# The opening of an agent-attention and expand-contract kernel, put in another order

## The chip, the cores and the metric

One of the eight cores of a Trainium2 chip runs the whole program. The metric is device time: microseconds from the start of the program to its end on that core. A time of a kernel is the median over several executions; one more execution is recorded by the hardware profiler, and all times inside the program come from that one.

A core has five engines with an instruction queue each, all in order: TensorE (PE in the profile; its weight loads have a row of their own, PEld), VectorE (DVE), ScalarE (ACT), GpSimd (POOL) and SyncE (SP), which here does nothing but start transfers. Sixteen DMA engines move the data.

## What is computed

Four batches; 12480 tokens of 128 numbers in each, 49 agents. First attention through the agents, then a layer that widens to 2048 and comes back:

```
s = scale * (a @ b.T);  e = exp(s - max(s));  sm(a, b) = e / (sum(e) + 1e-9)
agent_v = sm(agents, k) @ v                # 49 x 128 for each batch
x = sm(q, agents) @ agent_v                # one row for each token
h = x @ w_in                               # 128 -> 2048
out = (h - tanh(h)) @ w_out                # 2048 -> 128
```

`w_in` and `w_out` come as 64-bit floats and are turned into 32-bit floats on the chip ("decoding": six VectorE instructions and one on ScalarE for 512 columns).

## The kernel before

The inner products are reordered: `agent_v @ w_in` is made once for each batch (49 x 2048, "projection"), so that h is a product of the 49 weights of a token with it. h has 100 blocks of up to 500 tokens (`blocks`), and each block takes eight steps (`steps`, 256 of the 2048 columns each), 800 in all. A step is: `m1` (L563, h into PSUM, six matmuls), `tanh` and `square` on ScalarE (L573, L578), `mul` on VectorE (L583, g = h·z, which stands for h - tanh(h) at small h), and `m2` (L632, g times its part of w_out, added up in PSUM over the eight steps). In about two thirds of the steps g is split into a high part (GpSimd, L613) and a rest (VectorE, L618), so that `m2` can use fast 32-bit matmuls, twelve of them; the steps named in `PLAIN`, and all of block 0, take `m2` with g as it is, in eight passes of the slower form. Keys and values of batches 1 to 3 are worked on between the steps of the batch before; those of batch 0 have to come first. That is the opening, and it is what the change is about:

1. *Loads.* `fast` makes a list `loads`, and SP starts it in that order: 13 key tiles (`kt`, 512 KB each but the last) with the four parts of w_in (`raw`, 512 KB) in between, the first queries, 13 value tiles (`vt`), the second queries and the four parts of w_out. Keys and values share eight buffers (`K0`), so value tile j waits until TensorE is done with the tile that had its buffer. After the loads SP starts the small copies `pb<-pT` (L551, L552) that the first `m1` needs.
2. *Scores of batch 0* (`scores(g)` with b == 0, L273): eight 128-token tiles for a group, each a matmul with 128 columns of keys as weights and the agents of two batches, 98 columns, as the moving side; of those, 49 are used. ScalarE copies them (L284), VectorE takes the maxima (L286). In between VectorE decodes w_in (L175 to L185).
3. *Maximum* over all tokens (L314 to L334).
4. *Exponentials and values* (`av(g)`): VectorE subtracts the maximum (L344), ScalarE takes the exponential (L349), TensorE multiplies with the values (L380), and VectorE adds the exponentials up in two sums, one for even and one for odd groups (L399), added to each other at the end (L402). The first queries' softmax (`q_softmax`: L508, L514 to L529) and their transposition (L538, L547) stand in between.
5. *Quotient* (`sums`: L415 to L422) and the first parts of the projection (L472 to L476), among them, on VectorE, half of the decoding of the first part of w_out.
6. *Block 0*: its eight steps with the rest of the decoding of w_out and of the projection between them. Later in block 0 and at the start of block 1 `split_w_out` makes high and low parts of w_out, one quarter at each of the four positions in `SPLIT`: copies on ScalarE (L213, L218), difference on GpSimd (L214).

Order: VectorE and ScalarE run in the order in which the code is written from the end of the scores on (`issue_order(..., at)`), GpSimd and TensorE from the mark `early` on. Loads before `early` go first on SP.

The end: after the last block `low(0)` and `out` finish the last step, `take` and `finish` add the two halves of the result, and the last transfer carries blocks 98 and 99 together (L809).

Of the kernel before, what the change touches and what calls it, by code (L numbers as in the profile page):

```python
# [24 lines left out]
A = 49  # L25
# [9 lines left out]
GT = 8  # L35
# [29 lines left out]
SPLIT = (7, 4, 6, 8)  # L65
# [37 lines left out]
class Build:  # L103
# [95 lines left out]
    def load_w_in(self, c, raw):  # L199
        tiles = (self.work.tile([128, 512], F32, tag=t, name=t, bufs=2) for t in ("de", "rem", "da", "db"))  # L200
        run(self.decode(raw, self.w_in[:, c * 512 : (c + 1) * 512], *tiles))
# [6 lines left out]
    def split_w_out(self, c):  # L208
# [4 lines left out]
        nc.scalar.copy(h, w)  # L213
        nc.gpsimd.tensor_tensor(l, w, h.bitcast(F32), ALU.subtract)  # L214
        nc.gpsimd.memset(self.vb[c][:, :, C : C + 1], 1.0)
        for i, t in self.wo_f.items():
            if c == i // 2:
                nc.scalar.copy(t, w[:, 2 * C * (i % 2) :][:, : 2 * C])  # L218

    def phase1(self, b):  # L220
# [36 lines left out]
        def scores(g):  # L257
            yield
            if g == 0:
                st["s"] = self.keep.tile([128, NG * (GT + 1) * A], F32, tag="s", name="s", bufs=1)  # L260
                if b == 0:
                    st["mxp"] = self.work.tile([128, A, 2 * NG], F32, tag="mxp", name="mxp", bufs=1)
# [7 lines left out]
            if b == 0:  # L270
                ps = self.banks("h")
                for t in range(n):
                    nc.tensor.matmul(  # L273
                        ps[:, t // 4, (t % 4) * A2 : (t % 4 + 1) * A2],
                        kt[:, t, :],
                        self.ag[:, 0:2, :],
                        start=True,
                        stop=True,
                    )
                pv = ps[:, :, : 4 * A2].rearrange("p c (t a) -> p c t a", a=A2)[:, :, :, :A]  # L280
                for c in range(-(-n // 4)):
                    m = min(4, n - 4 * c)
                    sl = slice((g * GT + 4 * c) * A, (g * GT + 4 * c + m) * A)
                    nc.scalar.copy(st["s"][:, sl].rearrange("p (t a) -> p t a", a=A), pv[:, c, :m])  # L284
                banks = -(-n // 4)
                nc.vector.tensor_reduce(  # L286
                    st["mxp"][:, :, 2 * g : 2 * g + banks].rearrange("p a c -> p c a"),
                    pv[:, :banks, : min(4, n)].rearrange("p c t a -> p c a t"),
                    axis=AX.X,
                    op=ALU.max,  # L290
                )
                if g == EARLY - 1:
                    nc.vector.tensor_reduce(
                        st["mxp"][:, :, 2 * NG - 1], st["mxp"][:, :, : 2 * EARLY], axis=AX.X, op=ALU.max
                    )
                return
            ps = self.misc()
            for t in range(n):
                for r in range(0, 128, QUART):
                    to = ps[r : r + QUART, t * A : (t + 1) * A]  # L300
                    nc.tensor.matmul(to, kt[:, t, r : r + QUART], self.ag[:, b, :], start=True, stop=True)  # L301
            yield
            here = st["s"][:, g * GT * A : (g * GT + n) * A]
# [5 lines left out]
        def max_in():  # L309
# [3 lines left out]
            part = st["mxp"] if b else st["mxp"][:, :, 2 * EARLY :]  # L313
# [23 lines left out]
        def av(g, gaps=(0, 1)):  # L337
# [61 lines left out]
            nc.vector.tensor_tensor(es, e0, flat, ALU.add)  # L399
# [285 lines left out]
    def fast(self):  # L685
# [21 lines left out]
        with ExitStack() as first:  # L707
# [29 lines left out]
            for g in range(NG):  # L737
                run(p1[g])
                load(1)
                if g % 2 == 1 and 2 < g < 11:  # L740
                    self.load_w_in((g - 3) // 2, raws[(g - 3) // 2])
# [27 lines left out]
        early = self.count()  # L769
# [5 lines left out]
        rest0 = p1[2 * NG + 3 :]  # L775
        sums = rest0.pop(0)
        q1 = q_job(1)
        next(q1)
        for _ in range(3):
            next(sums)  # L780
        next(q1)
        go(dec[0], 3)
        run(sums)
        next(q1)
        run(rest0.pop(0))
        go(dec[0], 1)
        run(rest0.pop(0))
# [186 lines left out]
```

## Time and profile before

| what | value |
| --- | --- |
| median of three runs | 2018.5 us (2017.13 to 2018.8) |
| the profiled execution | 2018.59 us, its span 2016.8 us, 1.79 us lie around the span |
| TensorE busy | 1986.9 us of the span (99%) |
| VectorE, ScalarE, GpSimd busy | 1825.6, 1806.5, 999.9 us |
| the first 100 us: TensorE busy | 13.79, 17.81, 16.87, 16.53, 18.94 us in stretches of 20 us |

A row of a timeline reads: start in us, length in us, engine, line of the program, operation, output<-input, shapes, count, and in brackets how long the engine stood idle just before and what ended it. A row of the windows gives a stretch, its length, the busy time of PE, PEld, DVE, ACT and POOL (with counts), the granted TensorE clock as a share of full speed, the busy share of the DMA engines and what they moved in GB/s. A row of the waits reads: who waited, for whom, us in total, how often, the longest.

### The profile page before, as it was taken

The numbers are of one execution on the slowest core, as the hardware profiler recorded it, in microseconds if no ns is written. First come the engines' busy times: TensorE is split into PE (matmuls) and PEld (weight loads), VectorE is DVE, ScalarE is ACT, GpSimd is POOL, SyncE is SP. The second block draws the span as 40 slices with busy tenths as digits, with TensorE's granted clock in tenths as the row PEclk, the third lists the DMA queues.
The fourth block names the chain that finished last, engine by engine and source line by source line (L and its number), as shares of the span: only waits on it lengthen the run. The fifth ranks groups of instructions, "written<-read, shape, count | busy, mean of one in ns | idle before, by whom it ended". The sixth has DMA issues, their size and how long they took to land.

```text
span 2016.8 us, 49577 instructions
## 1 busy us (share of the span) xinstructions
PE 1986.9 (99%) x20779; PEld 1460.9 (72%) x20779; DVE 1825.6 (91%) x1986; ACT 1806.5 (90%) x2052; POOL 999.9 (50%) x702
## 2 busy tenths in 40 slices
PE   8899999999999999999999999999999999999998
PEld 7477767777677777777677777777767777777775
DVE  7799999889999998898999999889899999999997
ACT  3789989899999998899999999998999999999996
POOL 1254455555445455554454454555545546555554
PEclk9899999999999999999999999999999999999999
DMA  9422112221111222221012111221101101101100
GB/s 331 135 85 93 54 45 84 83 61 44 54 61 65 78 71 60 78 75 60 31 36 92 61 58 44 71 61 56 54 29 34 52 31 35 52 29 37 39 24 27
DMA packets 76601, 129.70 MB, mean 64 GB/s; under 512 B 5384, under 2 KB 55376, under 8 KB 76368
## 3 DMA queue, kind: packets, MB, share of 16 engines
q1 hardware_dynamic: 76368, 126.44, 19.2%
q8 instruction: 165, 2.70, 0.6%
q14 instruction: 68, 0.56, 0.1%
HBM read 81.10 MB, written 25.56 MB: 53 GB/s over the span
## 4 chain that ended last, share of the span: by engine, by line
PE 84%; ACT 8%; DVE 4%; issue 2%; DMA 1%; SPq 0%; POOL 0%; DVEq 0%; POOLq 0%
PE acc L632 49%; PE h L563 26%; ACT z L578 4%; ACT y L573 4%; DVE g L583 2%; PE misc L508 2%; PE misc L357 2%; PE pt L538 1%; PE misc L301 1%; PE h L273 1%; DVE gl L618 1%; PE misc L472 1%; DMA v<-w_out 1%; PE h L380 0%; ACT s L349 0%
## 5 line engine op out<-in xcount | busy, mean ns | idle before, releaser
L613 POOL TENSOR_SCALAR gh<-g 128x1000 fp32r<-128x1000 f32 (+1 forms) x545 | 853.0, 1565 | 622.5 <-DVE g L583 578.6
L583 DVE TENSOR_TENSOR g<-h,z 128x1000 f32<-128x1000 f32 (+1 forms) x800 | 955.5, 1195 | 133.5 <-ACT z L578 122.9
L573 ACT ACTIVATE y<-h 128x1000 f32<-128x1000 f32 (+1 forms) x800 | 802.4, 1003 | 68.6 <-PE h L563 60.5
L578 ACT ACTIVATE z<-y 128x1000 f32<-128x1000 f32 (+1 forms) x800 | 831.4, 1039 | 25.4
L618 DVE TENSOR_TENSOR gl<-g,gh 128x1000 fp32r<-128x1000 f32 (+1 forms) x545 | 656.8, 1205 | 1.3 <-POOL gh L613 1.0
L563 PE MATMUL h<-pT,awh 49*128 49x504 f32 x1600 | 552.0, 424 | 0.0
L632 PE MATMUL acc<-g,wo_f 64*128 64x500 f32 (+1 forms) x1960 | 443.3, 578 | 0.0
L632 PE MATMUL acc<-gh,wo_l 64*128 64x500 f32 (+1 forms) x2180 | 433.0, 387 | 0.5 <-POOL gh L613 0.2
L632 PE MATMUL acc<-gh,wo_h 64*128 64x500 f32 (+1 forms) x2180 | 432.6, 386 | 0.0
L563 PE MATMUL h<-pT,awl 49*128 49x504 f32 x800 | 369.5, 462 | 7.2 <-DVE awl L476 3.4
L632 PE MATMUL acc<-gl,wo_h 64*128 64x500 f32 (+1 forms) x2180 | 341.2, 387 | 1.0 <-DVE gl L618 0.5
L563 PE MATMUL h<-pb,awh 49*128 49x504 f32 x1600 | 317.1, 387 | 0.0
L563 PE MATMUL h<-pb,awl 49*128 49x504 f32 x800 | 309.0, 386 | 0.0
L632 PEld LDWEIGHTS acc<-g,wo_f 64*128 64x128 f32 x1960 | 190.6, 186 | 145.3 <-issue 126.1
L563 PEld LDWEIGHTS h<-pT,awh 49*128 49x128 f32 x1600 | 265.9, 186 | 20.9 <-issue 11.1
L632 PEld LDWEIGHTS acc<-gh,wo_h 64*128 64x128 f32 x2180 | 214.3, 186 | 37.2
L632 PEld LDWEIGHTS acc<-gl,wo_h 64*128 64x128 f32 x2180 | 211.5, 184 | 40.0 <-DVE gl L618 5.7
L632 PEld LDWEIGHTS acc<-gh,wo_l 64*128 64x128 f32 x2180 | 211.1, 184 | 38.6 <-POOL gh L613 1.7
L563 PEld LDWEIGHTS h<-pT,awl 49*128 49x128 f32 x800 | 147.6, 184 | 117.4 <-DVE o L641 49.9
L529 POOL TENSOR_TENSOR pp<-qe,pp 128x392 fp32r<-128x392 f32 x50 | 51.5, 1030 | 265.3 <-DVE pp L527 257.2
L563 PEld LDWEIGHTS h<-pb,awh 49*128 49x128 f32 x1600 | 153.9, 184 | 29.9 <-DMA pb<-pT 0.5
L563 PEld LDWEIGHTS h<-pb,awl 49*128 49x128 f32 x800 | 149.3, 187 | 11.7 <-issue 6.4
(113 smaller groups left out, 1130.4 us busy)
## 6 DMA issues: line engine op xcount, KB each, us to landing
kt<-kT SPq DMA_DIRECT2D x48, 512.0 KB
qt<-qT SPq DMA_DIRECT2D x46, 500.0 KB
outT<-o SPq DMA_DIRECT2D x46, 500.0 KB
pb<-pT SPq DMA_DIRECT2D x200, 96.5 KB
v<-v SPq DMA_DIRECT2D x36, 512.0 KB
vt<-v SPq DMA_DIRECT2D x12, 512.0 KB
raw<-w_in SPq DMA_DIRECT2D x4, 512.0 KB
v<-w_out SPq DMA_DIRECT2D x4, 512.0 KB
```

The source lines that it names most:

```text
L273: nc.tensor.matmul(ps[:, t // 4, (t % 4) * A2 : (t % 4 + 1) * A2], kt[:, t, :], self.ag[:, 0:2, :], start=True, stop=True,)
L301: nc.tensor.matmul(to, kt[:, t, r : r + QUART], self.ag[:, b, :], start=True, stop=True)
L357: nc.tensor.matmul(ps[HALF * odd : HALF * odd + w, : C + 1], flat[:r, t * A : t * A + w], vt[:r, t, : C + 1], start=t < 2, stop=t >= n - 2,)
L508: nc.tensor.matmul(to, qt[:, token : token + QUART], self.ag[:, b, :], start=True, stop=True)
L529: nc.gpsimd.tensor_tensor(pp[:, :, HALF:PW], ev, pp[:, :, :A].bitcast(F32), ALU.subtract)
L563: nc.tensor.matmul(h[:, c, : BT * TT], aw[a][rows[c], sl], pT[p][rows[c], :], start=k == 0, stop=k == 2)
L573: self.nc.scalar.activation(self.pair(y), h, AF.Tanh, scale=TSC)
L578: self.nc.scalar.activation(z, y, AF.Square, scale=GSC)
L583: self.nc.vector.tensor_tensor(self.pair(g), h, self.pair(z), ALU.mult)
L613: self.nc.gpsimd.tensor_scalar(gh, g, 1.0, 0.0, ALU.mult, ALU.add)
L618: self.nc.vector.tensor_tensor(gl, g, gh.bitcast(F32), ALU.subtract)
L632: nc.tensor.matmul(acc[:, r, :w], weights(c)[rows], g[rows, c * w : (c + 1) * w], start=i == 0 and k == 0, stop=i == NCH // 2 - 1 and k == ...
```

## The change

- *Scores.* The batch-0 scores are made as those of the other batches are: for each tile four matmuls with 32 tokens of keys as weights and the 49 agents of batch 0. One ScalarE copy and one VectorE maximum of 49 x 8 for a group, straight from PSUM.
- *Loads.* Two parts of w_in go between the keys, the other two between the values. They are decoded after the value products (part 2) and beside the quotient and the first projection (part 3).
- *Sums.* The odd groups' exponentials are added up on GpSimd instead of VectorE (five additions).
- *Quotient first.* Quotient and first projection stand ahead of the decoding of w_out, whose first half now follows them and whose second half comes after the first `mul`.
- *w_out.* The copies of `split_w_out` go from ScalarE to GpSimd, and two of the four positions move later (7 to 8, 8 to 9).
- *End.* Blocks 98 and 99 are stored one by one, and the very last step is a plain one: no high and low part.

Behind the scores the line numbers of the new kernel are 6 to 19 lower. The core of the diff:

```
-SPLIT = (7, 4, 6, 8)
+SPLIT = (8, 4, 6, 9)
...
-        nc.scalar.copy(h, w)
+        nc.gpsimd.tensor_scalar(h, w, 1.0, 0.0, ALU.mult, ALU.add)
...
-                nc.scalar.copy(t, w[:, 2 * C * (i % 2) :][:, : 2 * C])
+                nc.gpsimd.tensor_scalar(t, w[:, 2 * C * (i % 2) :][:, : 2 * C], 1.0, 0.0, ALU.mult, ALU.add)
...
-            if b == 0:
-                ps = self.banks("h")
-                for t in range(n):
-                    nc.tensor.matmul(
-                        ps[:, t // 4, (t % 4) * A2 : (t % 4 + 1) * A2],
-                        kt[:, t, :],
-                        self.ag[:, 0:2, :],
...
             ps = self.misc()
             for t in range(n):
                 for r in range(0, 128, QUART):
                     to = ps[r : r + QUART, t * A : (t + 1) * A]
                     nc.tensor.matmul(to, kt[:, t, r : r + QUART], self.ag[:, b, :], start=True, stop=True)
...
+            if b == 0:
+                nc.scalar.copy(here, ps[:, : n * A])
+                nc.vector.tensor_reduce(
+                    st["mxp"][:, :, g], ps[:, : n * A].rearrange("p (t a) -> p a t", a=A), axis=AX.X, op=ALU.max
+                )
...
-            nc.vector.tensor_tensor(es, e0, flat, ALU.add)
+            (nc.gpsimd if g % 2 else nc.vector).tensor_tensor(es, e0, flat, ALU.add)
...
-                if g % 2 == 0 and 0 < g < 10:
-                    loads.append((load_raw, g // 2 - 1))
+                if g in (2, 5):
+                    loads.append((load_raw, g // 3))
...
+                if g in (4, 8):
+                    loads.append((load_raw, 1 + g // 4))
                 loads.append((self.v0, g))
...
+            run(self.load_w_in(2, raws[2]))
+            early = self.count()
...
+            run(sums)
+            part = rest0.pop(0)
+            go(part, 3)
+            w3 = self.load_w_in(3, raws[3])
+            go(w3, 3)
+            run(part)
+            next(q1)
+            go(w3, 1)
+            run(rest0.pop(0))
+            run(w3)
...
         go(dec[0], 3)
-        run(sums)
-        next(q1)
-        run(rest0.pop(0))
-        go(dec[0], 1)
-        run(rest0.pop(0))
-        run(dec[0])
...
+            if n >= len(blocks) - 2:
+                nc.sync.dma_start(self.outT[:, column(n) : column(n) + width(n)], out_at(n))
...
-            plain = n == 0 or n % 2 * HP + i in PLAIN
+            plain = n == 0 or n % 2 * HP + i in PLAIN or k == len(steps) - 1
...
+            if k == 0:
+                run(dec[0])
...
+            if i == 0:
+                run(part)
```

On SP, the transfers of the opening in the new kernel, from the first keys to the last values (`raw` is a part of w_in):

```order
L235 DMA kt<-kT 128x1024 x2
L190 DMA raw<-w_in 128x512
L235 DMA kt<-kT 128x1024 x3
L190 DMA raw<-w_in 128x512
L235 DMA kt<-kT 128x1024 x7
L235 DMA kt<-kT 128x256
L476 DMA qt_99<-qT 128x1000
L246 DMA vt<-v 128x1024 x4
L190 DMA raw<-w_in 128x512
L246 DMA vt<-v 128x1024 x4
L190 DMA raw<-w_in 128x512
L246 DMA vt<-v 128x1024 x4
```

Before, all four parts of w_in stand among the first eight key tiles. The number of transfers and of bytes up to the last value tile is the same, and w_out and the copies `pb` follow as they did.

On VectorE before, from the last step of the quotient (`av<-avs`) to the second `mul` (`g<-h,z`); `gh`, `gl` and `awh<-gl` are the decoding of w_out here, `awl` the projection:

```order
L451 COPY av_95<-avs 128x49 x2
L476 TENSOR_TENSOR awl<-h,awh 113x256
L181 SCALAR_TENSOR_TENSOR gl<-v_90,gh 128x512
L476 TENSOR_TENSOR awl<-h,awh 113x512
L183 TENSOR_TENSOR gl<-gh,gl 128x512
L185 SCALAR_TENSOR_TENSOR awh<-gl 128x512
L583 TENSOR_TENSOR g<-h,z 128x1000
L175 TENSOR_SCALAR gh<-v_91 128x512
L177 SCALAR_TENSOR_TENSOR gh<-v_91,gh 128x512
L179 TENSOR_SCALAR gh<-gh 128x512
L476 TENSOR_TENSOR awl<-misc,awh 113x512
L583 TENSOR_TENSOR g<-h,z 128x1000
```

And the same place in the new kernel, where `da`, `db`, `rem` are the decoding of the last part of w_in:

```order
L179 TENSOR_SCALAR db<-da 128x512
L457 TENSOR_TENSOR awl<-h,awh 113x256
L496 TENSOR_REDUCE qm<-qe 128x8
L181 SCALAR_TENSOR_TENSOR rem<-raw,db 128x512
L457 TENSOR_TENSOR awl<-h,awh 113x512
L183 TENSOR_TENSOR rem<-da,rem 128x512
L185 SCALAR_TENSOR_TENSOR w_in<-de,rem 128x512
L175 TENSOR_SCALAR gh<-v_90 128x512
L177 SCALAR_TENSOR_TENSOR gh<-v_90,gh 128x512
L179 TENSOR_SCALAR gh<-gh 128x512
L564 TENSOR_TENSOR g<-h,z 128x1000
L181 SCALAR_TENSOR_TENSOR gl<-v_90,gh 128x512
```

The last three instructions of the first part of w_out have moved behind the first `mul`; part 3 of w_in stands where they stood.

On GpSimd in the new kernel, from the first queries' difference (`qe`) on; `es` are the sums of exponentials, `pp` the low part of the first queries' weights, `wo_h`, `wo_l`, `wo_f` the parts of w_out:

```order
L498 TENSOR_TENSOR qe<-qe,qm 128x392
L380 TENSOR_TENSOR es<-s 128x392
L380 TENSOR_TENSOR es<-es,s 128x392 x4
L510 TENSOR_TENSOR pp<-qe,pp 128x8x49
L213 TENSOR_SCALAR wo_h<-awh 128x512
L214 TENSOR_TENSOR wo_l<-awh,wo_h 128x512
L215 MEMSET v_91 128x8
L218 TENSOR_SCALAR wo_f_88<-awh 128x256
L498 TENSOR_TENSOR qe<-qe,qm 128x392
L213 TENSOR_SCALAR wo_h<-awh 128x512
```

Before, `pp` follows `qe` at once, and of each quarter of w_out only `wo_l` and the small fill stand here.

More of the change, by code (lines that the diff above doesn't have):

```diff
@@ L200, in load_w_in @@
         tiles = (self.work.tile([128, 512], F32, tag=t, name=t, bufs=2) for t in ("de", "rem", "da", "db"))
-        run(self.decode(raw, self.w_in[:, c * 512 : (c + 1) * 512], *tiles))
+        return self.decode(raw, self.w_in[:, c * 512 : (c + 1) * 512], *tiles)
     def load_w_out(self, c, raw):
@@ L261, in scores @@
                 if b == 0:
-                    st["mxp"] = self.work.tile([128, A, 2 * NG], F32, tag="mxp", name="mxp", bufs=1)
+                    st["mxp"] = self.work.tile([128, A, NG + 1], F32, tag="mxp", name="mxp", bufs=1)
                 else:
@@ L269, in scores @@
                 ahead("v", load_v, 0, g - NG + vb + 1)
-            if b == 0:
-                ps = self.banks("h")
-                for t in range(n):
-                    nc.tensor.matmul(
-                        ps[:, t // 4, (t % 4) * A2 : (t % 4 + 1) * A2],
-                        kt[:, t, :],
-                        self.ag[:, 0:2, :],
[L277 to L296, printed above, removed]
             ps = self.misc()
@@ L301, in scores @@
                     nc.tensor.matmul(to, kt[:, t, r : r + QUART], self.ag[:, b, :], start=True, stop=True)
+            here = st["s"][:, g * GT * A : (g * GT + n) * A]
+            if b == 0:
[3 more added lines that the diff above has]
+                )
+                if g == EARLY - 1:
+                    nc.vector.tensor_reduce(st["mxp"][:, :, NG], st["mxp"][:, :, :EARLY], axis=AX.X, op=ALU.max)
+                return
             yield
-            here = st["s"][:, g * GT * A : (g * GT + n) * A]
             nc.scalar.copy(here, ps[:, : n * A])
@@ L312, in max_in @@
             m = self.small.tile([128, A], F32, tag="m", name="m")
-            part = st["mxp"] if b else st["mxp"][:, :, 2 * EARLY :]
+            part = st["mxp"] if b else st["mxp"][:, :, EARLY:]
             nc.vector.tensor_reduce(m, part, axis=AX.X, op=ALU.max)
@@ L739, in fast @@
                 load(1)
-                if g % 2 == 1 and 2 < g < 11:
-                    self.load_w_in((g - 3) // 2, raws[(g - 3) // 2])
+                if g in (3, 7):
+                    run(self.load_w_in(g // 4, raws[g // 4]))
             at = self.count() - 1
@@ L768, in fast @@
                 run(av[g])
-        early = self.count()
+            run(self.load_w_in(2, raws[2]))
+            early = self.count()
+            rest0 = p1[2 * NG + 3 :]
+            sums = rest0.pop(0)
+            q1 = q_job(1)
+            next(q1)
+            for _ in range(3):
+                next(sums)
+            next(q1)
+            run(sums)
[4 more added lines that the diff above has]
+            run(part)
+            next(q1)
+            go(w3, 1)
+            run(rest0.pop(0))
+            run(w3)
         self.main = ExitStack()
@@ L774, in fast @@
         dec = [self.load_w_out(c, raws[4 + c]) for c in range(4)]
-        rest0 = p1[2 * NG + 3 :]
-        sums = rest0.pop(0)
-        q1 = q_job(1)
-        next(q1)
-        for _ in range(3):
-            next(sums)
-        next(q1)
-        go(dec[0], 3)
-        run(sums)
-        next(q1)
-        run(rest0.pop(0))
-        go(dec[0], 1)
-        run(rest0.pop(0))
-        run(dec[0])
+        go(dec[0], 3)
         live = []
```

2 lines of the change are left out of this document (1 added, 1 removed).

## The prediction

> **What bounds the kernel now.** First the windows, for where TensorE is full, and then the opening in windows of 4 us, for the DMA engines (last two columns: share, GB/s) and the granted clock (third from the end):
>
> ```profile
> 400.00:1000.00 600.00, 599.18 (x6353) 435.01 (x6351) 549.61 (x589) 547.14 (x616) 305.81 (x214) 1.00 0.20 62
> ...
> 32.00:36.00 4.00, 2.45 (x69) 2.04 (x71) 2.40 (x8) 0.65 (x2) 0.00 (x0) 0.64 1.03 406
> 36.00:40.00 4.00, 4.00 (x40) 4.00 (x42) 3.25 (x6) 2.25 (x6) 1.09 (x1) 0.51 0.37 86
> 40.00:44.00 4.00, 4.00 (x78) 4.00 (x75) 4.00 (x10) 3.95 (x10) 0.00 (x0) 1.00 0.89 288
> 44.00:48.00 4.00, 3.08 (x58) 2.84 (x54) 3.90 (x8) 0.52 (x1) 1.12 (x1) 1.00 0.94 315
> ...
> 56.00:60.00 4.00, 3.98 (x10) 1.73 (x10) 1.47 (x3) 0.96 (x2) 0.00 (x0) 0.50 1.03 266
> ...
> 64.00:68.00 4.00, 1.44 (x8) 1.19 (x10) 3.66 (x6) 3.94 (x6) 0.00 (x0) 0.90 0.52 170
> ```
>
> In the long stretch TensorE is full (599.18 of 600 us), and the change takes no work from it. So only the two ends can move: until TensorE is full, and after it has run dry. What reaches the full stretch earlier comes out of the total one for one. In the opening the DMA engines are full (1.03, 406 GB/s) but for a dip from 36 to 40 us, and not quite full to 48. The waits say why; the chain of waits and the timelines of TensorE and ScalarE say what hangs on it:
>
> ```profile
> SPq L246 <- PE h L380: 9.0, 5, 6.1
> ...
> PEld h L563 <- DMA pb<-pT: 0.5, 1, 0.5
> ...
> 46.64 12.14 DMA v<-w_out
> ...
> 59.85 0.74 PE L563 MATMUL h<-pb,awh 49*128 49x504 f32 x2
> ...
> 60.63 1.01 ACT L573 ACTIVATE y<-h 128x1000 f32<-128x1000 f32 x1 [1.11 <-PE h L563]
> ```
>
> Value tiles wait for TensorE to free a buffer, one of them 6.1 us: the dip. The last part of w_out lands at 46.64 + 12.14 = 58.78 us. The small copies `pb`, queued after it, land right behind: the first `m1` waits for them, its last matmuls begin at 59.85, and the first tanh at 60.63. So block 0 starts when the DMA queue has worked itself out. From there on VectorE is full, with `mul`s and decoding, as the window from 64 us shows (3.66 of 4; TensorE 1.44).
>
> **The change part by part.**
>
> *Scores.* TensorE's rows: the old form; the new form as batch 1 has it (64 instructions are a group of eight tiles); the same form at low clock; and VectorE's first subtraction:
>
> ```profile
> 6.21 25.15 PE L273 MATMUL h<-ag,kt 128*128 128x98 f32 x196 [6.21 <-DMA kt<-kT]
> ...
> 116.72 0.88 PE L301 MATMUL misc<-ag,kt 128*32 128x49 f32 x64
> ...
> 34.39 1.53 PE L508 MATMUL misc<-ag,qt 128*32 128x49 f32 x64
> ...
> 34.74 1.04 DVE L344 TENSOR_TENSOR s<-s,mb 128x392 f32<-128x392 f32 x2
> ```
>
> 196 instructions are 12.25 groups: 2.05 us a group now, 0.9 to 1.5 in the new form. A tile of 128 x 1024 x 4 bytes takes 1.29 us at 406 GB/s, so now the keys' arrival sets the pace. At 6.21 us the agents and the first tile are there; the other keys and two parts of w_in are 6.9 MB, another 17 us: TensorE ends at about 24, not at 31.36. Next late are the maxima on VectorE, new form (as batch 1 takes it, from SBUF) and old form (from PSUM):
>
> ```profile
> 118.66 0.87 DVE L305 TENSOR_REDUCE s<-s 128x49 f32<-128x392 f32 x1
> ...
> 15.81 0.56 DVE L286 TENSOR_REDUCE mxp<-h 128x98 f32<-128x392 f32 x1
> ```
>
> With 0.87 each and two parts of w_in decoded between them (six instructions each, at most 0.68 us as `L181` below) VectorE catches up from behind and ends some 1.5 us after TensorE. The Trainium skill (TensorEngine Tiling (Array Packing), Performance Considerations) warns of this: tiling speeds up TensorE and not the emptying of PSUM, which may become the bound. The trace agrees in so far as 0.87 us stand against the 1.29 of an arrival; with 0.56 the stage would end about a microsecond sooner, and nothing below would change.
>
> From TensorE's end to the first subtraction it is 34.74 - 31.36 = 3.4 us. So that comes at about 28.5 us (26.5 to 30, by the two prices), 6.2 earlier. The value tile that waited 6.1 us will find its buffer free while earlier transfers, the two late parts of w_in among them, still fill the engines to about 37 us: **the dip goes**. Its worth: against 406 GB/s there are missing 320 x 4, 118 x 4 and, to the last value at about 46.5 us, 91 x 2.5 us: 2.0 MB or 4.9 us. By the shares of the dip alone it would be 0.63 x 4 = 2.5. I take the bytes, since bytes are what must arrive, less something for the slowest engine: `pb` and the first tanh come **4.5 us earlier**, at 56.1 (bounds 2.5 and 5.0).
>
> *What else could hold the first tanh.* TensorE's last value products now, and the first projection:
>
> ```profile
> 48.64 2.53 PE L380 MATMUL h<-vt,s 128*64 128x128 f32 x36
> ...
> 56.02 2.88 PE L472 MATMUL h<-w_in,av 128*113 128x256 f32 x4 [1.47 <-DVE av L451]
> ```
>
> Up to the last value 14.9 MB follow the first key tile, 37 us: 43. From the end of the products to the projection it is 56.02 - 51.17 = 4.9 us, and less with the quotient first. The second queries' scores (1.53 us at low clock) stand ahead of the projection on TensorE and wait for a load that is two transfers behind the last value, 46 to 47. With 2.88 us for the projection that makes 43 + 4.9 + 1.5 + 2.9 = 52.3 at most, some 3 us before `pb`: covered. Under this cover lie also the two parts of w_in decoded late, and the five additions on GpSimd, priced by its nearest row:
>
> ```profile
> L529 POOL TENSOR_TENSOR pp<-qe,pp 128x392 fp32r<-128x392 f32 x50 | 51.5, 1030 | 265.3 <-DVE pp L527 257.2
> ```
>
> 5 x 1.03 = 5.2 us ahead of `pp` in GpSimd's queue. Begun at 31 they end before 37; the transposition that waits for `pp` stands behind the tenth value tile, at 41 or so. What VectorE is spared there nobody waits for. If `pb` were early and the cover gone, the late decoding would cost about 2 us.
>
> *Block 0 on VectorE.* From the first `mul` to the seventh, and one decoding instruction alone and beside GpSimd's work:
>
> ```profile
> 62.74 1.20 DVE L583 TENSOR_TENSOR g<-h,z 128x1000 f32<-128x1000 f32 x1 [1.17 <-ACT z L578]
> ...
> 74.29 0.68 DVE L181 SCALAR_TENSOR_TENSOR gl<-v,gh 128x512 f32<-128x512 uint32 x1
> ...
> 80.41 1.18 DVE L181 SCALAR_TENSOR_TENSOR gl<-v,gh 128x512 f32<-128x512 uint32 x1
> ...
> 82.96 2.30 DVE L583 TENSOR_TENSOR g<-h,z 128x1000 f32<-128x1000 f32 x2
> ```
>
> That is 20.2 us. Three more decoding instructions move in, 3 x 0.68 = 2.0, and about half of it goes into VectorE's own gaps there: **+1.0** (0 to 2). While VectorE waits for `pb` the order does not let it decode.
>
> *w_out's copies.* ScalarE loses eight; GpSimd's price for a copy is that of `gh`, alone and beside VectorE:
>
> ```profile
> L213 ACT CAST wo_h<-awh 128x512 fp32r<-128x512 f32 x4 | 2.4, 606 | 0.0
> L218 ACT COPY wo_f<-awh 128x256 f32<-128x256 f32 x4 | 1.5, 401 | 0.0
> ...
> 94.71 1.02 POOL L613 TENSOR_SCALAR gh<-g 128x1000 fp32r<-128x1000 f32 x1 [2.26 <-DVE g L583]
> 96.10 1.92 POOL L613 TENSOR_SCALAR gh<-g 128x1000 fp32r<-128x1000 f32 x1 [0.36 <-DVE g L583]
> ...
> 86.68 1.20 DVE L583 TENSOR_TENSOR g<-h,z 128x1000 f32<-128x1000 f32 x1
> ...
> 87.07 0.52 ACT L527 CAST pp<-qe 128x392 fp32r<-128x392 f32 x1
> ...
> 92.25 0.56 ACT L644 COPY o<-acc 128x500 f32<-128x500 f32 x1
> ...
> 92.84 0.68 DVE L641 TENSOR_TENSOR o<-o,acc 128x500 f32<-128x500 f32 x1 [2.05 <-ACT o L644]
> ...
> 93.57 0.49 PE L563 MATMUL h<-pT,awl 49*128 49x504 f32 x1 [0.78 <-DVE o L641]
> ```
>
> TensorE gets its full stretch at 93.57, 10.6 us behind the seventh `mul`, held by ScalarE. Without the copies the way is: two `mul`s and the second queries' quotient on VectorE, 86.68 - 82.96 = 3.7; then their cast 0.5, which ScalarE now waits for; four activations of 1.0; the result's halves 0.6 and 0.7: 9.5. So **-1.1** (0 to -3.9, all eight copies). On GpSimd a quarter of w_out costs its copies, 512 and 256 wide, 0.5 to 1.0 and 0.25 to 0.5, more than before, and three quarters run beside decoding. There they collide, as `L181` with 1.18 for 0.68 and `gh` with 1.92 for 1.02 show. Three such hits, less the one that is there now: **+1.0** (0 to 3.5, if seven were hit). The Trainium skill (GPSIMD Engine Reference, 1. Specifications) has the rule: GpSimd's way to SBUF is shared with VectorE and contends with its instructions that read two SBUF inputs. It speaks against this part, and both pairs of rows bear it out.
>
> *The end.*
>
> ```profile
> 2004.55 1.15 DVE L618 TENSOR_TENSOR gl<-g,gh 128x960 fp32r<-128x960 f32 x1
> ...
> 2007.79 0.73 PE acc L632 x4
> ...
> 1994.32 1.78 PE L632 MATMUL acc<-g,wo_f 64*128 64x480 f32 x8
> 1995.56 0.77 PE L563 MATMUL h<-pT,awl 49*128 49x504 f32 x1
> ...
> 2009.82 0.34 SPq L809 DMA_DIRECT2D outT<-o  x1
> ```
>
> The last step's plain form needs only its g. The step before it ends at 2005.70 + 0.73, then come 1.24 us (start to start of the plain rows): 2007.7 instead of 2008.5. The last transfer carries 480 columns instead of 980; 250 KB less at 406 GB/s are 0.6 us of the 7.0 from its start to the end of the span. Together **-1.4** (-0.8 to -2.2).
>
> *Sum:* -4.5 + 1.0 - 1.1 + 1.0 - 1.4 = -5.0 us. The profiled execution, 2018.59, becomes 2013.6; it lies 0.09 above the median of the runs shown, so the median is forecast at 2013.5. A change of 0.2%, 4.0 us, is about what a measurement of this kernel can tell from none; so "faster" begins below 2014.5, and the forecast lies only a microsecond beyond it.
>
> **The rivals.**
>
> *The dip only moves.* The value tile's wait of 6.1 us falls by what the first subtraction gains. Should the thirteen maxima and the twelve decoding instructions each take 0.17 us longer than priced, VectorE is 4.2 us later, the subtraction gains 2 us and not 6.2, and by the shares 2.5 x 2 / 6.1 = 0.8 us of the opening is left: 3.7 us more, 2017.2. For it: VectorE is the slow engine there, and w_out's rows move only 266 GB/s at a full share (56 to 60), so bytes may promise too much. Against it: VectorE has some 1.29 us for each arrival. Chance 0.24.
>
> *`pb` is not held behind w_out.* The copies are small and spread over few of the sixteen DMA engines; landing right behind w_out now may be chance. Then the projection, at about 52.3, sets the first tanh: 53.1, 7.5 us earlier, 3.0 more than forecast: 2010.5. For it: nothing but their size; against it: 58.78 and 59.85 lie only 1.1 us apart. Chance 0.13.
>
> *Slower: the clock stays down in block 0.* One `m2` at the low clock:
>
> ```profile
> 67.40 3.48 PE L632 MATMUL acc<-g,awh 64*128 64x500 f32 x8
> ```
>
> It takes 3.48 us for the 1.78 of full clock; with an `m1` some 4.7 us a step, where VectorE gives a step 20.2 / 6 = 3.4. Each such step costs 1.2 us; from five on the gain is gone (6.0 of 5.0), and all eight, 9.6, would give 2023.1. For it: with the dip filled, TensorE waits for `pb` with little to do, as in the window with 0.50, and VectorE, with more to do, leaves it idle between steps. Against it: at 64 to 68 the clock is granted at 0.90 with TensorE busy for 1.44 of 4 us only. The Trainium skill (TensorE: Matmul & The Clock Gate, Part 1) states the rule behind it: after a window of idleness TensorE runs at half its rate until it has been busy for a while. The 0.51 of the window from 36 us, behind a wait, agrees. Chance 0.07.
>
> **How the numbers follow.** The forecast has 0.56, the rivals 0.24, 0.13 and 0.07. The forecast's own range runs from the bounds of its terms, not all at one end: the opening 2.5 to 5.0, copies 0 to -3.9, collisions 0 to 3.5, the end -0.8 to -2.2: 2010.5 to 2017. With the first rival the range reaches up to 2018.0, with the second down to 2009.5; the third is left out. Of the forecast some 0.40 lies below 2014.5 and 0.15 above, with 0.01 over the other bound; the first rival is no change, the second faster: faster 0.53, same 0.39, slower 0.08.
>
> **What would show it.** Right: maxima that end near 26 us and a first subtraction at 27 to 30; no 4-us window under some 380 GB/s between 8 and 42 us; TensorE waiting for `pb`, and a first tanh near 56; 21 to 23 us from the first to the seventh `mul`; TensorE's full stretch from about 90; and an end 1.4 us nearer to the last step. Wrong: the first subtraction past 32 (the dip moves), `pb` landed well before the projection is done (second rival), a granted clock about 0.5 past 62 us (third), or `L181` rows mostly above 1.1 us in block 0, which would put the collisions at their upper end.

## The result, and the profile after

The new kernel takes 2031.97 us (median of four runs, 2031.51 to 2034.75), the kernel before 2017.82 in the same series: ratio 1.0075, interval 1.0062 to 1.0087, so it is 14 us slower. The profiled execution has a span of 2030.5 us, 13.7 more than before. TensorE reaches its full stretch at 107.6 us instead of 93.5, 14.1 us later: the whole loss and 0.4 us more. Stage by stage, from the starts and ends of the rows in the two traces (us):

| stage | before | after | difference |
| --- | --- | --- | --- |
| to the first subtraction of the maximum | 34.74 | 41.73 | +7.0 |
| from there to the end of the last value product | 16.4 | 22.8 | +6.4 |
| from there to the first tanh | 9.5 | 5.4 | -4.1 |
| first tanh to first `mul` | 2.1 | 3.4 | +1.3 |
| first to seventh `mul` | 20.2 | 24.8 | +4.6 |
| seventh `mul` to the full stretch | 10.5 | 9.5 | -1.1 |
| full stretch to the end of the span | 1923.3 | 1922.9 | -0.4 |

The full stretch is counted from the end of the addition on VectorE for which TensorE waits; TensorE's own row starts a few hundredths of a us later. Of the -4.1, 2.2 us lie ahead of the first projection (2.7 instead of 4.9) and 1.8 behind its start (2.8 instead of 4.6: it takes 1.51 instead of 2.88, and nothing waits for `pb`).

Half of the loss is there before the first subtraction, where 6.2 us were to be won. TensorE's timeline over the scores shows where:

```profile
5.49 2.84 PE L274 MATMUL misc<-ag,kt 128*32 128x49 f32 x128 [5.49 <-DMA kt<-kT]
9.76 2.18 PE L274 MATMUL misc<-ag,kt 128*32 128x49 f32 x95 [1.43 <-DMA kt<-kT]
13.15 2.25 PE L274 MATMUL misc<-ag,kt 128*32 128x49 f32 x97 [1.21 <-issue]
16.22 0.74 PE L274 MATMUL misc<-ag,kt 128*32 128x49 f32 x30 [0.82 <-DMA kt<-kT]
19.67 2.51 PE L274 MATMUL misc<-ag,kt 128*32 128x49 f32 x127 [2.71 <-issue]
25.89 2.84 PE L274 MATMUL misc<-ag,kt 128*32 128x49 f32 x127 [3.72 <-issue]
29.81 2.83 PE L274 MATMUL misc<-ag,kt 128*32 128x49 f32 x127 [1.08 <-issue]
36.83 1.36 PE L274 MATMUL misc<-ag,kt 128*32 128x49 f32 x53 [4.18 <-issue]
```

The last key tile lands at 24.1 us, but TensorE is done only at 38.2. Read the brackets and the counts together. (The profile has two records for each matmul of the scores; the counts here are of records, eight for a tile of keys instead of two.) From 17.0 us on it stands still for no key, no buffer and no other engine: the releaser is "issue", time in which it waited for nothing that the profile shows. And from the first stop on the runs between the stops are equally long: after the first 128 + 95 = 223 come 97 + 30 = 127, then 127, 127 and 127. That is no feature of the data, since a group has 64. The count is that of instructions: 127 matmuls with a weight load each are about 256 instructions. The DMA traffic of the first 45 us, of the new kernel and of the kernel before, has a row for them:

```profile
q8 instruction: 7, 0.11, 1.1%
```

```profile
q8 instruction: 3, 0.05, 0.4%
```

Seven packets of 16 KB instead of three. By the trace's records of single packets, those of the scores start at 10.81, 17.18, 23.45, 27.19 and 34.60 us and take 0.93 to 1.22; TensorE goes on at 13.15, 19.67, 25.89, 29.81 and 36.83, each time 1.3 to 1.4 us after a packet's end. It runs through one packet in 2.5 to 2.8 us, and the next starts 3.8, 1.3 and 4.8 us after the run has begun. The DMA engines meanwhile have their dip in the middle of the loads:

```profile
20.00:24.00 4.00, 2.17 (x116) 1.99 (x103) 1.14 (x2) 0.97 (x2) 0.00 (x0) 0.51 1.04 409
24.00:28.00 4.00, 2.11 (x104) 2.11 (x108) 0.53 (x1) 0.48 (x1) 0.00 (x0) 0.50 0.58 215
28.00:32.00 4.00, 2.92 (x143) 2.73 (x139) 1.18 (x3) 0.97 (x2) 0.00 (x0) 0.50 0.79 246
32.00:36.00 4.00, 0.65 (x32) 0.46 (x23) 1.28 (x2) 0.48 (x1) 0.00 (x0) 0.50 0.95 301
36.00:40.00 4.00, 1.71 (x54) 1.32 (x54) 1.04 (x3) 0.63 (x2) 0.00 (x0) 0.50 0.52 163
```

The value tiles wait for buffers that hold keys whose scores are not made (17.7 us in seven waits of SP, where the kernel before had 9.0 in five), so the dip did not go, it grew. The clock is granted at 0.50, VectorE (third pair) is idle for most of the time.

Of the rest, the rows after the first subtraction and in block 0 show the second part, first a row of the kernel before and then those of the new kernel:

```profile
37.23 5.67 DVE L344 TENSOR_TENSOR s<-s,mb 128x392 f32<-128x392 f32 x11
```

```profile
44.28 8.98 DVE L325 TENSOR_TENSOR s<-s,mb 128x392 f32<-128x392 f32 x11
...
59.81 4.69 PE L361 MATMUL h<-vt,s 128*64 128x128 f32 x36
...
73.29 1.19 DVE L564 TENSOR_TENSOR g<-h,z 128x1000 f32<-128x1000 f32 x1
...
82.67 1.28 POOL L214 TENSOR_TENSOR wo_l<-awh,wo_h 128x512 fp32r<-128x512 f32 x1
82.91 1.38 DVE L175 TENSOR_SCALAR gh<-v 128x512 uint32<-128x512 uint32 x1
...
92.78 1.58 POOL L214 TENSOR_TENSOR wo_l<-awh,wo_h 128x512 fp32r<-128x512 f32 x1
93.27 1.43 DVE L179 TENSOR_SCALAR gh<-gh 128x512 uint32<-128x512 uint32 x1
...
98.09 2.30 DVE L564 TENSOR_TENSOR g<-h,z 128x1000 f32<-128x1000 f32 x2
```

Eleven subtractions take 0.82 us each beside the sums on GpSimd; in the kernel before the same eleven take 0.52 each. Those are 3.3 of the 6.4 us. Another 2.9 lie in TensorE's work after it has waited 4.1 us for the low part `pp`: at a granted clock of 0.50 (60 to 64 us; 1.00 in the kernel before from 48 to 52) the transposition takes 1.73 us instead of 0.98, and the last 36 value products 4.69 instead of 2.53. In block 0 a decoding instruction takes up to 1.43 us instead of 0.43. TensorE does not wait for `pb` any more: it starts block 0 at 68.91 us, and the first two copies had landed at 62.7 and 63.6.

### The profile page after: what moved, and what is told of

The parts are those of the page before. It is cut to its first block, busy times and chain, and to the rows that moved or that the text cites. A ratio compares the mean times of both kernels' runs of the same rounds, so it can differ in the third digit from the quotient of the medians.

```text
span 2030.5 us, 50724 instructions
## 1 busy us (share of the span) xinstructions
PE 1980.8 (98%) x21363; PEld 1452.7 (72%) x21363; DVE 1828.6 (90%) x1980; ACT 1802.9 (89%) x2032; POOL 1008.5 (50%) x714
## 4 chain that ended last, share of the span: by engine, by line
PE 82%; ACT 9%; DVE 6%; issue 2%; DMA 1%; SPq 0%; POOL 0%; DVEq 0%; ACTq 0%
PE acc L613 48%; PE h L544 26%; ACT z L559 4%; ACT y L554 4%; DVE g L564 3%; PE misc L489 2%; PE misc L338 2%; PE misc L274 2%; PE pt L519 1%; DVE gl L599 1%; PE misc L453 1%; DMA kt<-kT 1%; DVE s L325 0%; ACT s L330 0%; DVE qe L505 0%
## 5 line engine op out<-in xcount | busy, mean ns | idle before, releaser
L544 PEld LDWEIGHTS h<-pb,awl 49*128 49x128 f32 x800 | 149.1, 186 | 14.1 <-issue 7.8
```

The lines of the kernel that those rows point to most:

```text
L544: nc.tensor.matmul(h[:, c, : BT * TT], aw[a][rows[c], sl], pT[p][rows[c], :], start=k == 0, stop=k == 2)
```

## The experiments

**Theory F:** TensorE runs out of instructions; its packets come slower than narrow tiles use them up. **Rivals:** L, the new order of the loads starves the scores; C, narrow tiles are slow in themselves, or their PSUM buffers are. For the rest, **theory P:** GpSimd's new work hinders VectorE at SBUF, against N, nobody waits there.

**64-token tiles.** The new kernel, with two matmuls for a tile of keys instead of four, so 392 weight loads instead of 784:

```
-                for r in range(0, 128, QUART):
-                    to = ps[r : r + QUART, t * A : (t + 1) * A]
+                step = QUART if b else HALF
+                for r in range(0, 128, step):
+                    to = ps[r : r + step, t * A : (t + 1) * A]
```

> The kernel after, with the scores of batch 0 in 64-token tiles: 392 weight loads with their matmuls. Theory F: some 170 more than the first 223, so one or two packets are waited for, and each was asked for early enough to come with the keys: the scores end at 25 to 28 us, the first subtraction is at 29 to 31 us and the time lies within 2 us of that with 128-token tiles. Rival C (the cost is that of narrow tiles): half of the loss stays, the scores end at about 31 us, the first subtraction is at about 35 us and the time is 5 to 7 us over that with 128-token tiles. Rival L: as with the 128-token tiles, 36 to 38 us.

2019.01 us against 2017.03 before in the same series, ratio 1.001 (1.000 to 1.002). The first subtraction is at 28.98 us. TensorE's timeline:

```profile
5.39 3.66 PE L275 MATMUL misc<-ag,kt 128*64 128x49 f32 x64 [5.39 <-DMA kt<-kT]
9.80 2.41 PE L275 MATMUL misc<-ag,kt 128*64 128x49 f32 x64 [0.76 <-DMA kt<-kT]
12.45 1.14 PE L275 MATMUL misc<-ag,kt 128*64 128x49 f32 x32 [0.24 <-DMA kt<-kT]
16.21 7.40 PE L275 MATMUL misc<-ag,kt 128*64 128x49 f32 x187 [2.62 <-DMA kt<-kT]
23.95 1.50 PE L275 MATMUL misc<-ag,kt 128*64 128x49 f32 x45 [0.34 <-issue]
```

It follows the keys and ends at 25.45. One stop for "issue" is left, 0.34 us, and it stands after 64 + 64 + 32 + 187 = 347 matmuls, nearly where the second stop for instructions stands in the new kernel, at 223 + 127 = 350. Loads, buffers, maxima and engines are those of the new kernel, so L falls. C falls too: between its stops the new kernel makes 127 matmuls in 2.5 to 2.8 us, 0.16 to 0.18 us for the eight of a tile, as much as the four of a tile take here (16.0 us for 98 tiles). So 13 us of the loss (1.0075 to 1.001) hang on the number of instructions in the scores. The five stops of the new kernel add up to 12.9 us.

**Narrow tiles on the kernel before.** Only the scores of the change, with the old order of the loads:

```
-                ps = self.banks("h")
...
-                        kt[:, t, :],
-                        self.ag[:, 0:2, :],
...
             ps = self.misc()
             for t in range(n):
                 for r in range(0, 128, QUART):
                     to = ps[r : r + QUART, t * A : (t + 1) * A]
                     nc.tensor.matmul(to, kt[:, t, r : r + QUART], self.ag[:, b, :], start=True, stop=True)
```

> The kernel before, with the scores of batch 0 in 32-token column tiles and nothing else of the change: the order of the loads is the old one. Theory F: the same 784 weight loads with their matmuls run out of instructions at the same places; the scores end at 36 to 39 us (31.4 in the kernel before), the first subtraction comes at 40 to 43 us instead of 34.7, and the time rises by 3 to 7 us over the kernel before, part of it hidden behind the transfers of w_out. Rival L: the scores end at 25 to 27 us and the time is that of the kernel before or up to 4 us less. Rival C: as F.

2025.2 us, ratio 1.0038 (1.0024 to 1.0052): 8 us slower, a little more than expected, and the first subtraction at 39.83. The stops stand where they stand in the new kernel, after 223 matmuls and every 127:

```profile
9.85 2.27 PE L274 MATMUL misc<-ag,kt 128*32 128x49 f32 x95 [1.71 <-DMA kt<-kT]
13.23 0.94 PE L274 MATMUL misc<-ag,kt 128*32 128x49 f32 x33 [1.11 <-issue]
15.05 2.16 PE L274 MATMUL misc<-ag,kt 128*32 128x49 f32 x94 [0.87 <-DMA kt<-kT]
21.02 2.83 PE L274 MATMUL misc<-ag,kt 128*32 128x49 f32 x127 [3.81 <-issue]
27.29 2.84 PE L274 MATMUL misc<-ag,kt 128*32 128x49 f32 x127 [3.44 <-issue]
```

**128-token tiles with 49 columns.** As the first, with one matmul for a tile (`step = QUART if b else 128`):

> The kernel after, with the scores of batch 0 in 128-token tiles again but 49 moving columns: 196 weight loads with their matmuls instead of 784. Theory F (TensorE runs out of instructions: they come in packets of 16 KB, some 127 weight loads with their matmuls, and a packet queued among the key transfers takes about 6 us while the scores use one up in 2.5 to 2.9): 196 stay below the first 223 that ran without a stall, so the scores end within 2 us of the last key (24.1 us), the first subtraction comes at 28 to 30 us instead of 41.7, and the time falls by 9 to 13 us to 2019 to 2023. Rival L (the new order of the loads starves the scores): the scores end at 36 to 38 us again and the time stays at 2030 to 2034. Rival C (the column tiles themselves, or their PSUM buffers, are slow): as F here.

A miss: 2042.16 us, ratio 1.0122 (1.0105 to 1.0138). There is no stop, as F has it, but the matmuls are slow:

```profile
5.52 42.02 PE L275 MATMUL misc<-ag,kt 128*128 128x49 f32 x196 [5.52 <-DMA kt<-kT]
```

That is 0.43 us a tile at a clock of 1.00, where the old form with 98 columns takes 0.256. The run says nothing against F, but it gives no time for "narrow tiles undone" either.

**784 weight loads in wide tiles.** The same, and three small matmuls ahead of each tile's own, whose results are written over:

```
+                for _ in range(0 if b else 3):
+                    nc.tensor.matmul(ps[:QUART, t * A : t * A + 1], kt[:, t, :QUART], self.ag[:, b, :1], start=True, stop=True)
```

> The kernel after, with the scores of batch 0 in 128-token tiles and 49 moving columns, and ahead of each tile's matmul three small ones (32 tokens as weights, one moving column) whose results are written over: 784 weight loads with their matmuls again, in wide tiles. Theory F: the stalls come back after about 223 and then every 127; the scores end at 35 to 40 us, the first subtraction comes at 39 to 43 us and the time is 2029 to 2035 us. Rival C: as the 128-token tiles without the small ones, the first subtraction at 28 to 31 us. Rival L: the same as in all runs with the new order, 36 to 38 us for the end of the scores.

Another miss: 2096.61 us, and no stop for "issue" in 784 matmuls. A tile takes 1.0 us here, from one of these rows to the next:

```profile
6.19 0.66 PE L277 MATMUL misc<-ag,kt 128*128 128x49 f32 x2
...
7.19 0.66 PE L277 MATMUL misc<-ag,kt 128*128 128x49 f32 x2
```

With eight matmuls to a tile, a packet's 127 last about 16 us, and the packets start some 16 us apart (18.01, 32.88, 49.24, 64.96). The number of instructions alone does not stall TensorE; it is the number in a time. F holds in the narrower form: 127 in less time than a packet takes to come.

**Sums back on VectorE**, on the version with 64-token tiles:

```
-            (nc.gpsimd if g % 2 else nc.vector).tensor_tensor(es, e0, flat, ALU.add)
+            nc.vector.tensor_tensor(es, e0, flat, ALU.add)
```

> The kernel after with 64-token tiles, and the odd groups' sums of exponentials back on VectorE. Theory P (GpSimd's additions and VectorE's subtractions hinder each other at SBUF: 0.82 us for each of eleven subtractions, where the kernel before has 0.52): the eleven take 5.7 us again, the low part pp and the transposition come 2.5 to 3.5 us earlier after the first subtraction (16.4 us to 13 or 14), the last value product ends at 46 to 48 us instead of 50.3, and as VectorE has five additions more (2.7 us) the time falls by 1 to 3 us against the 64-token version. Rival N (as the prediction had it: nobody waits there): the subtractions stay at 0.8 us, or are faster without a gain; the time stays within 0.5 us or rises by up to 2.7 us.

2016.6 us against 2017.40 before in the same series, ratio 0.9995 (0.9985 to 1.0004); with the sums on GpSimd it was 2019.01, in another series. The eleven subtractions have their old price, and the last value product ends at 45.82 us instead of 50.31:

```profile
31.89 5.67 DVE L326 TENSOR_TENSOR s<-s,mb 128x392 f32<-128x392 f32 x11
```

So the hindrance is shown. The gain is not: the first tanh is at 56.70 (55.82 with the sums on GpSimd) and the full stretch begins at 93.46 (93.44). VectorE decodes a part of w_in before it takes up the value products, and TensorE, idle for those 2.98 us, makes the projection at low clock in 2.90 us instead of 1.51. The 2.4 us between the medians do not lie in the opening; from the full stretch to the last addition the profiled executions of all versions differ by up to 2 us (1914.3 to 1916.4).

**Copies of w_out back on ScalarE**, on the same version:

```
-        nc.gpsimd.tensor_scalar(h, w, 1.0, 0.0, ALU.mult, ALU.add)
+        nc.scalar.copy(h, w)
```

(and the same for `wo_f`)

> The kernel after with 64-token tiles, and the copies of w_out back on ScalarE (at the four new positions). Theory P: the decoding instructions that took 0.76 to 1.43 us beside the copies (0.42 to 0.69 alone) go back to their own times but for one or two; from the first to the seventh product it takes 21.3 to 22.5 us instead of 24.8, from the seventh to the full stretch 10 to 11.5 us instead of 9.5, and the time falls by 1 to 3 us against the 64-token version. Rival S (ScalarE is the bound in block 0): the copies lengthen the tanh and square chain by as much, the full stretch begins at 93 to 94 us as it does now, and the time stays within 0.5 us.

2017.78 us, ratio 1.0003 (0.9994 to 1.0013). From the first to the seventh `mul` it takes 22.0 us instead of 24.8, and only one decoding instruction is still hindered:

```profile
70.15 0.42 DVE L175 TENSOR_SCALAR gh<-v 128x512 uint32<-128x512 uint32 x1
...
77.14 1.68 POOL L214 TENSOR_TENSOR wo_l<-awh,wo_h 128x512 fp32r<-128x512 f32 x1 [31.82 <-ACT wo_h L213]
77.72 1.43 DVE L179 TENSOR_SCALAR gh<-gh 128x512 uint32<-128x512 uint32 x1
```

What hinders it is not a copy but GpSimd's difference `wo_l` (L214), which was on GpSimd in the kernel before as well. With the copies on GpSimd the first three of these differences begin at 68.6, 76.5 and 78.7 us, with the copies on ScalarE at 77.1, 83.2 and 89.5; VectorE decodes until 82.55, so only the first still meets it. From the seventh `mul` to the full stretch it is 11.4 us instead of 9.5. So the copies cost 2.7 us on GpSimd, by the time at which they let the differences run, and save 1.9 on ScalarE: 0.8 lost, or nothing within what the runs can tell.

**64-token tiles alone on the kernel before**, nothing else of the change:

> The kernel before, with the scores of batch 0 in 64-token tiles of 49 columns, their maxima in one reduction for a group, and nothing else of the change. Theory: with no stall for instructions, no GpSimd beside VectorE and no decoding moved into block 0, the scores end at 28 to 29.5 us, the first subtraction comes at 31 to 32.5 us, the transfers go on without the dip at 36 to 40 us, the first tanh is at 55 to 58 us and TensorE's full stretch begins at 88 to 91 us: 3 to 5 us less than the kernel before, 2012 to 2015 us. Rival W (the queue ends with w_out no earlier, so pb and the first tanh stay): the first tanh is at 59.5 us or later and the time lies within 1 us of the kernel before.

2015.52 us against 2017.40, ratio 0.9992 (0.9983 to 1.0001). The opening does what was expected: first subtraction 31.47, first tanh 57.07, full stretch at 89.9 instead of 93.5, and the dip of 86 GB/s is gone:

```profile
36.00:40.00 4.00, 3.96 (x74) 3.72 (x72) 4.00 (x10) 4.00 (x10) 0.00 (x0) 1.00 1.03 406
```

Of these 3.6 us the medians show 1.9, and the interval still touches 1. The time lies just outside what was expected.

**And the change's end on top** (blocks 98 and 99 stored one by one, a plain last step):

> The version with 64-token tiles alone on the kernel before, and the change's end on top (blocks 98 and 99 stored one by one, the last step plain). Theory: the opening is the same to 0.3 us, and from the start of TensorE's full stretch to the end of the span it takes 1922.0 to 1922.6 us instead of 1923.3: 0.7 to 1.4 us less than without, 2011 to 2014.5 us. Rival: the last step's eight slow matmuls take what the missing steps give, and the time is the same within 0.3 us.

2014.34 us against 2017.40, ratio 0.9988 (0.9979 to 0.9997); 1.2 us under the version without the end, less than the intervals of the two can tell apart. From the start of the last addition to the end of the span it is 6.7 us instead of 7.3 without.

**And the quotient first**, with the three decoding instructions of w_out behind the first projection's start:

```
-        go(dec[0], 3)
         run(sums)
+        part = rest0.pop(0)
+        go(part, 3)
         next(q1)
-        run(rest0.pop(0))
+        go(dec[0], 3)
+        run(part)
```

> The version with 64-token tiles and the change's end, and of the quotient-first part this: the quotient and the start of the first projection stand ahead of the first three decoding instructions of w_out on VectorE, which stay ahead of the first product. Theory: the quotient waits for these three (1.5 us) in the versions without; the scaled agent values come 1.4 to 1.7 us earlier, at 50.5 to 51.5 us, the first tanh 1 to 1.6 us earlier, and the time is 0.8 to 1.6 us less than without: 2012 to 2014.5 us. Rival V (VectorE is the bound there all the same): the three instructions stand ahead of the first product as before, the first product comes no earlier, and the time is the same within 0.4 us. Rival P (pb lands at 53 to 55 us and holds the first matmuls): TensorE waits for pb and the gain is under 0.5 us.

2012.28 us against 2017.41, ratio 0.9975 (0.9965 to 0.9986). The same kernel once more, from which its profile is:

> The same kernel as the one with the quotient first, once more, for a profile at the undisturbed clock and a second interval. Theory: as measured before, a median of 2011 to 2014 us, 0.15 to 0.35% under the kernel before; the first tanh at 55 to 56.5 us and the full stretch from 87.5 to 89 us. Rival: the gain was the draw of one round, and the ratio lies within 0.1% of one.

2012.03 us against 2017.88, ratio 0.9972 (0.9961 to 0.9983). In its profile the projection's first four matmuls take 1.51 us, at full clock, where they take 2.88 in the kernel before, and the rows on which the first tanh and the full stretch stand are:

```profile
55.29 0.49 PE L545 MATMUL h<-pT,awl 49*128 49x504 f32 x1 [1.45 <-DVE awl L458]
...
89.19 0.49 PE L545 MATMUL h<-pT,awl 49*128 49x504 f32 x1 [0.78 <-DVE o L623]
```

The first tanh is at 56.29, the full stretch 4.4 us earlier than before. TensorE now waits for VectorE (1.45 us), not for `pb`. This version is 5.8 us faster than the kernel before. The steps that lead to it, 1 to 2 us each, have intervals that overlap from one version to the next; against the kernel before, those of the last two lie well clear of 1.

**What makes wide tiles slow.** On the version with the end, scores in 128-token tiles with 64 moving columns, in one PSUM bank:

> The version with 64-token tiles and the change's end, but with the scores of batch 0 in 128-token tiles with 64 moving columns (49 of batch 0 and 15 of batch 1 that nobody uses): 196 weight loads with their matmuls. A 128-token tile took 0.256 us with 98 moving columns and 0.43 us with 49. Theory A (there is a least number of moving columns between 49 and 64 below which a matmul with a full weight load takes twice as long): a tile takes 0.17 to 0.26 us and the scores end at 26 to 31 us, the time is within 2 us of the version with 64-token tiles. Theory B (the time goes by something else, such as the place in PSUM or a clock): a tile takes 0.4 us or more, the scores end at 45 us or later and the time rises by 12 us or more.

Theory A falls: 42.0 us for 196 again, 2035.4 us in all. So with 49 columns in the kernel before's two banks:

> The version with 64-token tiles and the change's end, but with the scores of batch 0 in 128-token tiles with 49 moving columns, written to the two banks of PSUM that the kernel before uses (four tiles in each) instead of the one bank. A tile took 0.256 us there with 98 columns, and 0.43 us in one bank with 49 and with 64. Theory D (the one bank is what makes it slow): a tile takes 0.26 us or less, the scores end at 24 to 31 us, the time is within 2 us of the version with 64-token tiles. Theory E (the number of moving columns is what decides): 0.43 us a tile again, the scores end at about 47 us, and the time is 2033 to 2038 us.

2035.67 us, and the group of the scores reads, beside it that of the kernel before:

```profile
L274 PE MATMUL h<-ag,kt 128*128 128x49 f32 x196 | 42.0, 413 | 5.4 <-DMA kt<-kT 5.4
```

```profile
L273 PE MATMUL h<-ag,kt 128*128 128x98 f32 x196 | 25.1, 297 | 6.2 <-DMA kt<-kT 6.2
```

The bank is not it. What is left is the number of moving columns, and with it how far apart the results lie in PSUM. 64 columns were tried in one bank only; the step lies between 64 and 98. Why is open.

## Why the prediction was wrong

**The scores: the step that failed.** "196 instructions are 12.25 groups: 2.05 us a group now, 0.9 to 1.5 in the new form", so "the keys' arrival sets the pace" and "TensorE ends at about 24". The 0.88 us is the price of one group of batch 1, 64 matmuls that stand between the longer matmuls of the steps; in that long stretch TensorE has 6353 matmuls in 600 us, some 127 in 12 us. Thirteen such groups in a row use instructions faster than they come, and the supply is no row of the timeline: it shows as "issue" in a profile that has it, and not at all in one whose TensorE is slower. In the kernel before, 196 matmuls and as many weight loads in 25 us used up a packet and a half. What could have warned: the number of instructions went from 196 to 784, and the profile has a queue of its own for instructions that shares the DMA engines, which were full. No rival of the prediction was about it. With 64-token tiles the same steps come out as forecast: end of TensorE 25.45 (about 24), first subtraction 28.98 (28.5). That the first tanh comes at 55.82 (56.1) is luck: in that run the first copies `pb` had landed at 51.5 and 52.2, and VectorE's projection rows set it.

That the packets are late because they stand behind key transfers is argued: they start 3.8 and 4.8 us after a run begins where the engines are busy for 0.79 to 1.04 of the time, and 1.3 us after at 0.58. The share alone does not settle it: with narrow tiles on the kernel before, a packet starts 3.9 us after its run has begun beside full engines (1.02), and another 1.3 us after between windows of 1.03 and 0.79. It was not tried apart, and stays open. The Trainium skill (Runtime: NRT & Kernel Launch, Instruction fetch mechanics) has blocks of 16 KiB or 256 instructions, and says of crossing such a boundary that its cost is mostly hidden. The packets of 16 KB and the runs of 127 agree with the first; here the crossing was not hidden, it cost 1.1 to 4.2 us five times over.

**The dip** did not go, for the reason above; on 64-token tiles it does. **`pb`:** the prediction had TensorE wait for it at about 56. It waited for VectorE instead, in the new kernel and in all versions with 64-token tiles. The second rival named this sign, but its mechanism is not what happened: the first copies land right behind the last part of w_out or together with it in every trace (58.78, then 58.85 and 59.80 in the kernel before; 62.95, and 62.73 and 63.63 in the new one; 52.08, and 51.52 and 52.20 with 64-token tiles). What changed is that with 64-token tiles the queue is done 6.7 us earlier, more than the 4.5 of the forecast, while the projection's chain came at 55 and not at 52.3.

**"What VectorE is spared there nobody waits for"** failed as a step: it priced the additions on GpSimd and not what they do to VectorE beside them, although the prediction used just that for the copies: 3.3 us on eleven subtractions, on the way to the last value product. What it concluded for the time is not refuted: with the sums back on VectorE the full stretch begins at the same time.

**Block 0:** mis-sized. The moved decoding and the collisions were forecast at +1.0 and +1.0, +2.0 from the first to the seventh `mul`; it was 4.6; by the run with the copies back on ScalarE the collisions made 2.7 of it, and 1.9 are left. Some 0.5 of these is the one hit that is still there in that run; that the rest is the price of the moved instructions is argued. Ahead of the first `mul` another 1.3 us were lost to three decoding instructions that were to hide behind the wait for `pb`. No `L181` was hit (0.68 each). The hits were on `L175` (1.38 twice, for 0.42), `L179` (0.95 and 1.43, for 0.43) and `L177` (0.76 and 0.97, for 0.69), and the four large ones (0.95 to 1.43) lie not beside the copies but beside GpSimd's differences, `wo_l` three times and `qe` once, which the copies put at another time. **From the seventh `mul` on:** -1.1 forecast, -1.1 measured.

**The end:** -1.4 forecast. From the last addition to the end -0.9, and from the last-but-one step's last matmuls to the copy of the result 2.4 us instead of 2.8: -1.3 together. That the table has only -0.4 lies in the long stretch, which differs from one execution to the next.

**The rival for "slower"** is not what happened: the clock was low in the scores (0.50 from 20 to 40 us), and in block 0 no 4-us window has it under 0.76. With 64-token tiles it is 1.00 from 20 to 28 us, so the low clock went with the stops.

## What to carry to other kernels

Before matmuls are cut into more and smaller ones, count the instructions of the stretch and divide by its time: here TensorE kept up with one packet of 127 weight loads and matmuls in 16 us and lost 1.1 to 4.2 us a packet at 127 in 2.8 us beside busy DMA engines (0.58 to 1.04). A price measured on a short burst is not the price of a long run of such bursts. And what goes to GpSimd is priced by what it does to VectorE's rows beside it and by when it lets GpSimd's later work run, not by its own row alone.

## What the runs showed of the hardware

- TensorE's instructions arrive in packets of 16 KB, and after one has landed it takes 1.3 to 1.4 us until the first matmul of it runs, in the new kernel and with narrow tiles on the kernel before.
- A 128-token tile of f32 weights takes 0.43 us with 49 moving columns, in one bank or two, and with 64 in one bank, and 0.256 us with 98 in two: fewer columns were slower. Two 64-token halves with 49 columns take 0.16 us together (16.0 us for 392 records, four to a tile).
- VectorE's shift-and-mask instruction (`L175`) takes 0.42 us alone and 1.38 beside GpSimd's difference, three times as long, although it reads one input only. It ends shortly after GpSimd's row: with `wo_l` ending at 83.95 and 91.89, the two hit rows end at 84.29 and 92.23, 0.34 us later; three hit `L179` rows (two of the new kernel, one of the version with the copies on ScalarE) end 0.28 to 0.34 us after theirs. The two-input `L177` goes from 0.69 to 0.76 and 0.97. The rule that the prediction cites (GPSIMD Engine Reference, 1. Specifications, of the Trainium skill) names a second kind, instructions in a 2-port performance mode. 512 numbers in 0.42 us may be that kind; no run here tells it apart.
